# A second, unread result on some VectorE comparisons in an FNet block with a routed feed-forward row

## The chip, the cores and the metric

The kernel runs on one core of one Trainium2 chip. The metric is the device time of one execution in microseconds (us). A change of less than about 2 us (1%) can't be told from none here.

## The reference

```python
h  = x + A(layernorm(x))          # x: [2048, 576] f32
#   A(z) = Re( DFT_seq( DFT_hid(z) ) ), both DFTs given as full cos/sin matrices
h2 = h + B(layernorm(h))
#   B(z): r = z @ w_r; take the one row with the largest r;
#         y = (silu(z_row @ w_gate) * (z_row @ w_up)) @ w_down * sigmoid(r_row)
#         return z, with y added at that row
# seq matrices 2048x2048 (re, im), hid matrices 576x576 (re, im),
# w_gate, w_up 576x4608, w_down 4608x576, all f32
```

## The kernel before, in words

The sequence DFT is done by symmetry: of each 2048-row matrix only some blocks of columns are used in matmuls. A program that relied on the symmetry without looking would be wrong for other inputs, so the kernel also loads the other blocks and compares them with their mirror images: a difference is written as bf16 into a buffer `Q` (two slots), ScalarE squares it and adds it up (`add_square`, L368), and at the end a sum above zero sends the program into a general path that is not run here.

A block `C[j, i, False]` comes straight by a DMA of SP's queue (`load_c`, L357). Its mirror image `C[j, i, True]` has its rows in reverse order, so it comes by an indirect DMA, a gather, whose descriptors GpSimd (POOL) makes (`gather`, L301; 32 such gathers of the sequence matrices, 3 of the hidden matrices, 4 of `x`). Four functions on VectorE (DVE) compare: `off_s` (L375, a block with its mirror), `off_t` (L380, block `NK - j` with block `j` reversed), `off_h` (L387, halves of a block, a subtraction and an addition) and `off_w` (L422 to L427, the hidden matrices). All are `tensor_tensor` with both inputs f32 in SBUF. When a comparison has read its buffer, the buffer goes back to a ring of seven `RAW` and some `D` buffers, and the next load or gather into it can be issued. Between the comparisons DVE also does the steps of the transform: `keep` (L583, one input in PSUM), `residual` (L619) and `dot_h` (L623), the last two with a sum (`accum_out`), which the engine returns by an extra instruction, DVE_READ_ACCUMULATOR.

The order of all this work is written out by a small planner, `Plan`: each step is added with its engine, a duration in us and the steps it depends on; `order()` simulates the engines and returns the steps by start time, and the program is emitted in that order. The dependencies themselves are kept by semaphores. `load` (L705) adds a load on SP or POOL; `c_half`, `c_check` and `w_check` add the comparisons. The feed-forward weights (`load_ffn`, L1200) follow on SP's queue, into buffers as they come free.

Of the kernel before, what the change touches and what calls it, by code (L numbers as in the profile page):

```python
# [7 lines left out]
F32 = mybir.dt.float32  # L8
# [3 lines left out]
OP = mybir.AluOpType  # L12
AX = mybir.AxisListType

P = 128
S = 2048
D = 576
F = 4608
NK = S // P
# [51 lines left out]
class Plan:  # L71
# [3 lines left out]
    def __init__(self):  # L75
        self.ops = []

    def add(self, eng, dur, fn, *deps, tail=0.0, push=0.0):
        flat = []
        for d in deps:  # L80
            flat += d if isinstance(d, list) else [d]
        n = {"eng": eng, "dur": dur, "fn": fn, "deps": [d for d in flat if d], "tail": tail, "push": push}
        n["i"] = len(self.ops)
        self.ops.append(n)
        return n

    def order(self):
        HOP = 0.15
        succ = [[] for _ in self.ops]
        for n in self.ops:  # L90
            for d in n["deps"]:
                succ[d["i"]].append(n)
        for n in reversed(self.ops):
            n["way"] = n["dur"] + n["tail"] + max((m["way"] for m in succ[n["i"]]), default=0.0)
        left = [len(n["deps"]) for n in self.ops]
        open_ = {}
        for n in self.ops:
            n["at"] = 0.0
            if not n["deps"]:
                open_.setdefault(n["eng"], []).append(n)  # L100
        free = {}
        done = []
        while any(open_.values()):
            best = None
            for eng, ns in open_.items():
                if not ns:
                    continue
                t = max(free.get(eng, 0.0), min(n["at"] for n in ns))
                n = min(
                    (n for n in ns if n["at"] <= t + 1e-9),  # L110
                    key=lambda n: (n["at"] if eng == "DMA" else -n["way"] - n["push"], n["i"]),
                )
                if best is None or t < best[0]:
                    best = (t, n)
            t, n = best
            open_[n["eng"]].remove(n)
            n["start"], n["end"] = t, t + n["dur"]
            free[n["eng"]] = n["end"]
            done.append(n)
            for m in succ[n["i"]]:  # L120
                hop = 0.0 if m["eng"] == n["eng"] else HOP
                m["at"] = max(m["at"], n["end"] + n["tail"] + hop)
                left[m["i"]] -= 1
                if not left[m["i"]]:
                    open_.setdefault(m["eng"], []).append(m)
        assert len(done) == len(self.ops)
        return sorted(done, key=lambda n: (n["start"], n["i"]))


class Slots:  # L130
# [12 lines left out]
def kernel(  # L143
# [13 lines left out]
    pe, act, dve, pool, sp = nc.tensor, nc.scalar, nc.vector, nc.gpsimd, nc.sync  # L157
# [23 lines left out]
    mp = main.enter_context(tc.tile_pool(name="main", bufs=1))  # L181
# [4 lines left out]
    eps = consts.tile([P, 1], F32, name="eps")  # L186
# [153 lines left out]
    C, DT = {}, {}  # L340
# [28 lines left out]

    SIGN = (OP.subtract, OP.add)  # L370

    def off_s(j, i, u, n):

        o = Q[:, u % 2, n * 7 * P : (n + 1) * 7 * P].rearrange("p (k m) -> p k m", m=P)
        dve.tensor_tensor(o, C[j, i, True][:, 0:7, :], C[j, i, False][:, 7:0:-1, :], op=SIGN[i])  # L375

    def off_t(j, i, u):

        o = Q[:, u % 2, 14 * P : QW].rearrange("p (k m) -> p k m", m=P)
        dve.tensor_tensor(o, C[NK - j, i, False], C[j, i, False][:, :, ::-1], op=SIGN[i])  # L380

    def off_h(g, c, n, i, u):

        o = Q[:, u % 2, i * 9 * n * HM : (i + 1) * 9 * n * HM].rearrange("p (c k m) -> p c k m", k=9, m=HM)
        t = DT[g, i][:, c : c + n]
        for k, op in enumerate((OP.subtract, OP.add)):
            dve.tensor_tensor(o[:, :, k::2, :], t[:, :, k::2, 0:HM], t[:, :, k::2, HM:P], op=op)  # L387

    def square(u, w, ps=P):
        add_square(Q[0:ps, u % 2, 0:w])  # L390
# [26 lines left out]
    def off_w(n, u):  # L417

        ps = W_ROWS[n]
        t, o = WM["ABC"[n]][0:ps], Q[0:ps, u % 2]  # L420
        re, im = W["ABC"[n]][0:ps, 0, :], W["ABC"[n]][0:ps, 1, :]
        dve.tensor_tensor(o[:, 0:D], t[:, 0:D], re[:, 0:D], op=OP.subtract)  # L422
        dve.tensor_tensor(o[:, D : 2 * D], t[:, D : 2 * D], im[:, 0:D], op=OP.add)
        o = o[:, 2 * D : 3 * D]
        dve.tensor_tensor(o[:, 0:287], re[:, 1:HD], re[:, D - 1 : HD : -1], op=OP.subtract)
        dve.tensor_tensor(o[:, 287:575], im[:, 1 : HD + 1], im[:, D - 1 : HD - 1 : -1], op=OP.add)
        dve.tensor_copy(o[:, 575:576], im[:, 0:1])  # L427
# [264 lines left out]
    plan = Plan()  # L692
    add = plan.add

    def then(f, *args):
        return lambda: f(*args)
# [8 lines left out]
    def load(eng, f, mb, *deps):  # L705

        ns = in_flight[eng]
        n = add(eng, 0.1 if eng == "SP" else 1.3, f, *deps, ns[-8:-7])
        d = add("DMA", mb / 0.405, None, n, moved[-1:])
        moved.append(d)  # L710
        ns.append(add("COME", 0.0, None, d, tail=1.8))
        return n, ns[-1]
# [4 lines left out]
    def in_turn(eng, f, mb, *deps):  # L717
        LAST[eng], d = load(eng, f, mb, LAST[eng], *deps)
        return d
# [6 lines left out]
    for k, n in X_LOADS:  # L726
        d = in_turn("SP" if k < 9 else "POOL", then(load_x, k, n), 0.295 * n)
# [11 lines left out]
    for a, b in X_RUNS:  # L739
        ks = ORDER[a:b]  # L740
        push = 8.0 if a == 14 else 0.0
        e = add("POOL", 0.6, then(ends, a, b), [CAME[k] for k in ks])
        r = [add("DVE", 0.84, then(fold_d, k), CAME[k]) for k in ks]
        m = [add("ACT", 0.95, then(measure, k), f, push=push) for k, f in zip(ks, r)]
        o = add("POOL", 0.3, then(totals, a, b), e, m)
# [3 lines left out]
        o = add("POOL", 2.0, then(biases, a, b), r, o)  # L749
# [23 lines left out]
    for k in FOLDED:  # L773
        dg, use, at = [], [], []
        for sl in slots_of(k):
            n = next(places)
            UF[sl] = LATER[n]
            at.append(PLACE[n])
            if k in PAIRS:
                u, w = dgs.take()  # L780
                dg.append(add("DVE", 0.17, then(diag, sl, u), MEAS[sl], w, IDENT))
                use.append(u)
        if k in PAIRS:
            of = ys if k % 2 else zs
            (y0, w0_), (y1, w1_) = of.take(), of.take()
            f = pe_last = add("PE", 1.95, then(fold, k), dg, w0_, w1_, pe_last)
# [45 lines left out]
    def c_half(g, c, m):  # L832
        u, w = qs.take()
        cus = [[CU[j, i, False] for j in GROUPS[g][c : c + m]] for i in range(2)]
        n = [
            add("DVE", 0.16 + 0.62 * m, then(off_h, g, c, m, i, u), [d for _, d in cus[i]], w)
            for i in range(2)
        ]
        for i in range(2):
            for b, _ in cus[i]:  # L840
                users[b].append(n[i])
        squares(u, 9 * m * P, n)

    def squares(u, w, n, ps=P):
        SQUARES.append(add("ACT", 0.3 + w / 1200, then(square, u, w, ps), n))
        qs.users[u].append(SQUARES[-1])

    def c_check(j, i):

        u, w = qs.take()  # L850
        u0, d0 = CU[j, i, False]
        c_load(j, i, True)
        u1, d1 = CU[j, i, True]
        n = [add("DVE", 1.08, then(off_s, j, i, u, 0), d0, d1, w)]
        users[u0] += n
        users[u1] += n
        free.append(u1)
        if j in PAIRS:
            m = NK - j
            c_load(m, i, False)  # L860
            c_load(m, i, True)
            (u2, d2), (u3, d3) = CU[m, i, False], CU[m, i, True]
            n.append(add("DVE", 1.08, then(off_s, m, i, u, 1), d2, d3, w))
            users[u3].append(n[1])
            n.append(add("DVE", 1.36, then(off_t, j, i, u), d0, d2, w))
            users[u0].append(n[2])
            users[u2] += n[1:]
            free.extend([u3, u2])
        if u0[0] == "D1":
            free.append(u0)  # L870
        squares(u, QW if j in PAIRS else 7 * P, n)

    WS, WL, WRAP = [], [], []
# [8 lines left out]
    def w_check():  # L882
        for n in range(3):
            u, d = ring("POOL", load_w, (0.59, 0.59, 0.16)[n], n + 3)
            q, w = qs.take()
            o = add("DVE", 2.2, then(off_w, n, q), WL[n], d, w)
            users[u].append(o)
            squares(q, 3 * D, o, W_ROWS[n])
            WS.append(o)
            free.append(u)  # L890
# [259 lines left out]
    o = add("DVE", 1.0, check_sum, SCORES, SQUARES, xs_is)  # L1150
    o = add("PE", 0.3, check_all, o)
# [6 lines left out]
    for b in range(NJ // TW):  # L1158
        j = TW * b
# [186 lines left out]
    after, best = {}, None  # L1346
    for _ in range(N_PLAN):
        end, todo, next_ = plan_ffn(after)
        if best is None or end < best[0]:
            best = end, after  # L1350
        after = next_
    for n in plan_ffn(best[1])[1]:
        if n["fn"]:
            n["fn"]()
    main.close()


    with tc.If(T["mv"], preferred_fallthrough_block=False):
        with ExitStack() as gen:
# [33 lines left out]
            with ExitStack() as hs:  # L1393
# [9 lines left out]
                with tc.For_i(0, NK, 1) as k:  # L1403
                    dve.tensor_copy(xr, row_of(GX, k))
                    norm(xn, xr, "x")
                    for a in range(5):
                        w = min(P, D - a * P)
# [4 lines left out]
                    for c in range(4):  # L1412
                        pa = zbank(f"gpa{c}")
                        for a in range(5):
                            w = min(P, D - a * P)
                            pe.matmul(
                                pa[:, :HD], xt[0:w, a, :], GW[0:w, a, c * HD : (c + 1) * HD],
                                start=(a == 0), stop=(a == 4),
# [8 lines left out]
            with tc.For_i(0, NK, 1) as j:  # L1427
                dve.tensor_copy(hn, row_of(GX, j))
                with tc.For_i(0, 2 * NK, NB) as k0:
# [7 lines left out]
                    for k in range(NB):  # L1437
                        for c in range(2):
                            pe.matmul(
                                ps[c][:, :HD], gc[:, k, :], gk[:, k, half(c)],  # L1440
                                start=(k == 0), stop=(k == NB - 1),
# [89 lines left out]
```

## Time and profile before

| | |
|---|---|
| median of 3 runs | 199.22 us (198.27, 199.22, 199.5) |
| the profiled execution | 199.04 us |
| its span, first to last instruction | 197.4 us |
| moved by DMA | 77.81 MB, 394 GB/s over the span |
| busy: DVE, ACT, PE, POOL | 84%, 71%, 66%, 59% |

The span is what the trace shows; 1.64 us of the profiled execution lie around it. Busy shares are means over stages that differ. POOL's busy time includes the time that a gather is held up, since a held gather shows as a long one.

### The profile page before, as it was taken

To read this page: it belongs to the slowest core of one execution; us is meant where nothing else is said; L and a number is where in the kernel's file an instruction comes from. 1 tells how busy PE (TensorE), PEld (TensorE's weight loads), DVE (VectorE), ACT (ScalarE), POOL (GpSimd) and SP (SyncE) were. 2 spreads that over 40 slices of the span, in tenths; PEclk is the share of its full clock that TensorE was granted. 3 is DMA by queue.
4 is the path that set the end of the run, shared out by engine and by line. 5 is a ranking of instruction groups with operands and counts; after the bars stand their busy time and mean duration, and the time that the engine had idled before them with its cause. 6 is when DMAs were issued, how large, how long until landed. Compare 5 with 4: busy or idle time off the path is not lost. (4 is left out here: it accounts for less than half of the span.)

```text
span 197.4 us, 2794 instructions
## 1 busy us (share of the span) xinstructions
PE 129.6 (66%) x758; PEld 89.9 (46%) x758; DVE 166.6 (84%) x419; ACT 140.4 (71%) x259; POOL 117.2 (59%) x139
## 2 busy tenths in 40 slices
PE   0007999999999999799999986900232036263940
PEld 0005667754667788477876764700121013031430
DVE  4399996999899968999799999999947999989720
ACT  3198853684699578799389399889555999877630
POOL 6488888284637876359780000003874999999900
PEclk9999999999999999999999999975555555558797
DMA  5999999999899999999999999999999999999992
GB/s 171 408 418 412 413 409 406 411 381 330 281 405 411 411 363 402 400 410 411 416 405 414 418 424 420 426 422 412 424 431 425 420 428 424 422 431 414 412 427 99
DMA packets 14587, 77.81 MB, mean 394 GB/s; under 512 B 1951, under 2 KB 1955, under 8 KB 11239
## 3 DMA queue, kind: packets, MB, share of 16 engines
q1 hardware_dynamic: 10461, 56.56, 71.5%
q0 software_dynamic: 4096, 21.03, 26.5%
q8 instruction: 7, 0.11, 0.2%
q14 instruction: 13, 0.11, 0.1%
q10 hardware_dynamic: 10, 0.00, 0.0%
HBM read 72.86 MB, written 6.49 MB: 402 GB/s over the span
## 5 line engine op out<-in xcount | busy, mean ns | idle before, releaser
L368 ACT ACTIVATE Q<-Q 128x2944 bf16<-128x2944 bf16 (+5 forms) x26 | 55.4, 2132 | 18.5 <-DVE Q L380 8.9
L610 PE MATMUL py<-W,Z 128*128 128x289 f32 x180 | 45.4, 409 | 3.8 <-DVE X L619 3.8
L565 PE MATMUL ps<-D,XF 128*128 128x320 f32 (+3 forms) x216 | 45.0, 408 | 0.5 <-DVE Z L583 0.5
L301 POOL DMA_INDIRECT R<-in_ct_dram,ic x21 | 32.1, 1528 | 17.7 <-DVE Q L375 13.5
L610 PEld LDWEIGHTS py<-W,Z 128*128 128x128 f32 x180 | 33.6, 189 | 15.2 <-issue 4.5
L565 PEld LDWEIGHTS ps<-D,XF 128*128 128x128 f32 (+1 forms) x216 | 32.0, 172 | 13.0 <-issue 1.5
L1228 POOL TENSOR_TENSOR D<-D,Z 128x1152 f32<-128x1152 f32 x8 | 20.9, 2642 | 0.0
L676 POOL DMA_DIRECT2D out_dram<-X x1 | 0.6, 621 | 32.1 <-ACT X L661 32.1
L301 POOL DMA_INDIRECT D<-in_ct_dram,ic x11 | 13.8, 1250 | 7.6 <-DVE Q L380 4.6
L498 ACT ACTIVATE junk<-X,XT 128x576 bf16<-128x576 f32 x16 | 12.3, 771 | 7.8 <-DMA X<-in_x_dram 3.3
L1233 ACT ACTIVATE junk<-D 128x576 bf16<-128x576 f32 x20 | 13.7, 683 | 3.2 <-POOL D L1228 2.6
L1255 PE MATMUL pd<-XF,H 128*1 128x144 f32 x80 | 5.3, 439 | 14.6 <-DVE H L1247 11.3
L537 PE MATMUL fo<-W,diag 128*128 128x288 f32 (+1 forms) x8 | 4.2, 706 | 16.3 <-DVE diag L528 16.3
L375 DVE TENSOR_TENSOR Q<-R,D 128x896 bf16<-128x896 f32 x11 | 11.9, 1084 | 3.2 <-DMA D<-in_ct_dram 1.8
L387 DVE TENSOR_TENSOR Q<-D 128x640 bf16<-128x640 f32 (+3 forms) x20 | 12.8, 691 | 1.7 <-DMA W<-in_wt_dram 1.7
L380 DVE TENSOR_TENSOR Q<-R,D 128x1152 bf16<-128x1152 f32 x10 | 13.4, 1348 | 0.0
L630 ACT ACTIVATE junk<-X,TD 128x576 bf16<-128x576 f32 x16 | 12.3, 766 | 1.4 <-DVE X L619 1.3
L661 ACT ACTIVATE X<-X,BB,UP 128x576 f32<-128x576 f32 x14 | 10.8, 854 | 3.1 <-DVE BB L642 3.1
L623 DVE SCALAR_TENSOR_TENSOR junk<-X,wr 128x576 bf16<-128x576 f32 x16 | 12.1, 755 | 0.3
L375 DVE TENSOR_TENSOR Q<-D 128x896 bf16<-128x896 f32 x11 | 11.8, 1082 | 0.0
L619 DVE SCALAR_TENSOR_TENSOR X<-py,X 128x576 f32<-128x576 f32 x16 | 11.6, 748 | 0.0
L375 DVE TENSOR_TENSOR Q<-R 128x896 bf16<-128x896 f32 x10 | 10.7, 1082 | 0.1
(205 smaller groups left out, 260.8 us busy)
## 6 DMA issues: line engine op xcount, KB each, us to landing
D<-in_ct_dram SPq DMA_DIRECT2D x22, 576.0 KB
R<-in_ct_dram SPq DMA_DIRECT2D x10, 576.0 KB
D<-in_wu_dram SPq DMA_DIRECT2D x5, 1152.0 KB
D<-in_wd_dram SPq DMA_DIRECT2D x4, 1152.0 KB
R<-in_wg_dram SPq DMA_DIRECT2D x3, 1152.0 KB
D<-in_wg_dram SPq DMA_DIRECT2D x3, 1152.0 KB
out_dram<-X SPq DMA_DIRECT2D x2, 1440.0 KB
X<-in_x_dram SPq DMA_DIRECT2D x4, 576.0 KB
```

Source lines behind the costliest of these rows:

```text
L301: pool.indirect_dma_start(tile, None, view, bass.IndirectOffsetOnAxis(ap=rows, axis=0), element_offset=at)
L368: act.activation(t, t, AF.Square, accum_out=DS[0 : t.shape[0], n : n + 1])
L375: dve.tensor_tensor(o, C[j, i, True][:, 0:7, :], C[j, i, False][:, 7:0:-1, :], op=SIGN[i])
L380: dve.tensor_tensor(o, C[NK - j, i, False], C[j, i, False][:, :, ::-1], op=SIGN[i])
L387: dve.tensor_tensor(o[:, :, k::2, :], t[:, :, k::2, 0:HM], t[:, :, k::2, HM:P], op=op)
L498: act.activation(junk[:, 0:D], X[:, k, 0:D], AF.Square, bias=XT[:, n : n + 1], scale=-float(D), accum_out=VX[:, n : n + 1],)
L565: pe.matmul(cm(ZP[g, n][k % 2][p0 : p0 + m], w), XF[:, q, m0 : m0 + m], DT[g, i][:, :, k, 0:HM], start=k in (0, 1), stop=k in (6, 7),)
L610: pe.matmul(YP[GROUPS[g][c]][:, h, 0:w], Z[:, a, c * P : (c + 1) * P], w_block(a)[:, h * HD : h * HD + w], start=(a == 0), stop=(a == 4),)
L623: dve.scalar_tensor_tensor(junk2, X[:, k, 0:D], 1.0, wr, op0=OP.mult, op1=OP.mult, accum_out=TD[:, n, 0:1])
L630: act.activation(junk[:, 0:D], X[:, k, 0:D], AF.Square, bias=TD[:, n, 1:2], scale=-float(D), accum_out=VAR[:, n : n + 1],)
L1228: pool.tensor_tensor(t, t, xs.unsqueeze(1).to_broadcast([P, JW, D]), op=OP.mult)
L1233: act.activation(junk[:, 0:D], WB[w, j][:, r, :], AF.Copy, accum_out=acc[:, j + r : j + r + 1])
```

## The change

A step can now be marked `holds` (the comparisons of `c_half`, `c_check` and `w_check`) or `moves` (the loads). After the planner has made its order, `apart` goes through the loads on POOL's queue: it looks for the DVE step `a` that is running, by the planner's own times, when the load starts. If `a` holds, the pair of `a` and its successor and the next pair after that are looked at, and the first of a pair is noted if both hold and less than 0.2 us lie between them. The order is made before that and stays as it is; no load, buffer or wait on another engine is changed by the code of the diff.

A noted comparison is emitted as `scalar_tensor_tensor` (multiply by 1.0, then the same subtraction or addition) with `accum_out` into a new two-column tile `spill` that nobody reads. This brings a DVE_READ_ACCUMULATOR behind it. `off_h` keeps its two `tensor_tensor` and gets between them a product of one column, also with a sum. In `off_w` only the first of five operations takes part.

```diff
+    def apart(self, todo):
+        ops = [n for n in todo if n["eng"] == "DVE"]
+        found = set()
+        for n in todo:
+            if n["eng"] != "POOL" or not n["moves"]:
+                continue
+            for k, (a, b) in enumerate(zip(ops, ops[1:])):
+                if a["start"] <= n["start"] + 0.0 < a["end"] and a["holds"]:
+                    for a, b in list(zip(ops, ops[1:]))[k : k + 2]:
+                        if a["holds"] and b["holds"] and b["start"] - a["end"] < 0.2:
+                            found.add(a["i"])
+        return found
...
+    spill = mp.tile([P, 2], F32, name="spill")
+    open_ = [False]
+    def differ(o, a, b, op):
+        if open_[0]:
+            dve.scalar_tensor_tensor(o, a, 1.0, b, op0=OP.mult, op1=op, accum_out=spill[:, 0:1])
+        else:
+            dve.tensor_tensor(o, a, b, op=op)
+    def pause():
+        dve.scalar_tensor_tensor(
+            spill[:, 1:2], eps, 1.0, eps, op0=OP.mult, op1=OP.mult, accum_out=spill[:, 0:1]
+        )
...
-        dve.tensor_tensor(o, C[j, i, True][:, 0:7, :], C[j, i, False][:, 7:0:-1, :], op=SIGN[i])
+        differ(o, C[j, i, True][:, 0:7, :], C[j, i, False][:, 7:0:-1, :], SIGN[i])
...
-        dve.tensor_tensor(o, C[NK - j, i, False], C[j, i, False][:, :, ::-1], op=SIGN[i])
+        differ(o, C[NK - j, i, False], C[j, i, False][:, :, ::-1], SIGN[i])
...
             dve.tensor_tensor(o[:, :, k::2, :], t[:, :, k::2, 0:HM], t[:, :, k::2, HM:P], op=op)
+            if open_[0] and k == 0:
+                pause()
...
-        dve.tensor_tensor(o[:, 0:D], t[:, 0:D], re[:, 0:D], op=OP.subtract)
+        differ(o[:, 0:D], t[:, 0:D], re[:, 0:D], OP.subtract)
...
-    for n in plan_ffn(best[1])[1]:
+    todo = plan_ffn(best[1])[1]
+    apart = plan.apart(todo)
+    for n in todo:
         if n["fn"]:
+            open_[0] = n["i"] in apart
             n["fn"]()
```

## Rows read from the trace of the kernel before

**Rows 1.** The table by stretch: start and end of the stretch and its length in us, busy time of each engine (and its instructions), the granted TensorE clock, the mean busy share of the 16 DMA engines, and what they moved. A share may read slightly above 1.

```profile
44.00:48.00 4.00, 4.00 (x31) 1.99 (x29) 3.48 (x5) 2.00 (x5) 0.94 (x1) 1.00 1.04 288
...
50.50:54.00 3.50, 3.50 (x15) 2.47 (x14) 2.55 (x5) 2.91 (x3) 2.26 (x2) 1.00 0.81 237
54.00:72.00 18.00, 18.00 (x74) 13.41 (x73) 16.09 (x19) 15.13 (x18) 11.92 (x9) 1.00 1.02 410
...
76.00:104.00 28.00, 26.47 (x126) 20.68 (x126) 26.23 (x42) 21.45 (x27) 18.21 (x14) 1.00 1.02 409
104.00:172.00 68.00, 32.36 (x204) 21.27 (x198) 62.79 (x172) 55.20 (x113) 30.99 (x29) 0.69 1.01 422
172.00:192.00 20.00, 11.88 (x196) 6.33 (x196) 14.35 (x47) 12.78 (x38) 15.40 (x6) 0.76 1.02 422
```

**Rows 2.** The timeline of SP's queue, from three windows: start and length in us, line, operation, target and source; the last row is the last load of feed-forward weights.

```profile
41.72 0.33 SPq L357 DMA_DIRECT2D R<-in_ct_dram  x1
51.02 0.33 SPq L357 DMA_DIRECT2D R<-in_ct_dram  x1
171.09 0.33 SPq L1202 DMA_DIRECT2D W<-in_wd_dram  x1
```

**Rows 3.** Who waited for whom, SP's queue, 44 to 52 us: total, times, longest.

```profile
SPq L357 <- DVE Q L380: 8.9, 1, 8.9
```

**Rows 4.** POOL's timeline, gathers only: start, length; in brackets the idle time before it and what ended that.

```profile
39.69 4.30 POOL L301 DMA_INDIRECT R<-in_ct_dram,ic  x1 [3.49 <-DVE Q L375]
44.29 0.94 POOL L301 DMA_INDIRECT R<-in_ct_dram,ic  x1 [0.30 <-DVE bt L737]
48.20 1.55 POOL L301 DMA_INDIRECT R<-in_ct_dram,ic  x1 [2.96 <-DVE Q L375]
50.06 1.76 POOL L301 DMA_INDIRECT R<-in_ct_dram,ic  x1 [0.31 <-DVE Z L583]
52.12 0.95 POOL L301 DMA_INDIRECT R<-in_ct_dram,ic  x1 [0.30 <-issue]
55.23 1.55 POOL L301 DMA_INDIRECT R<-in_ct_dram,ic  x1 [2.16 <-DVE Q L375]
...
88.20 4.33 POOL L301 DMA_INDIRECT R<-in_ct_dram,ic  x1 [0.30 <-issue]
...
95.75 1.29 POOL L301 DMA_INDIRECT R<-in_ct_dram,ic  x1 [0.30 <-issue]
```

**Rows 5.** DVE's timeline beside the first of these gathers and up to the fifth, in the same columns. Lengths of neighbours overlap by 0.08 us; the time that an operation takes is from its start to the next start.

```profile
39.34 1.08 DVE L375 TENSOR_TENSOR Q<-R 128x896 bf16<-128x896 f32 x1
40.34 1.35 DVE L380 TENSOR_TENSOR Q<-R,D 128x1152 bf16<-128x1152 f32 x1
41.61 1.55 DVE L387 TENSOR_TENSOR Q<-D 128x320 bf16<-128x320 f32 x4
43.09 0.88 DVE L583 SCALAR_TENSOR_TENSOR Z<-ps,os 128x320 f32<-128x320 f32 x2
...
44.57 1.09 DVE L375 TENSOR_TENSOR Q<-R,D 128x896 bf16<-128x896 f32 x1 [0.52 <-ACT Q L368]
...
49.65 1.34 DVE L380 TENSOR_TENSOR Q<-R,D 128x1152 bf16<-128x1152 f32 x1
50.91 1.08 DVE L375 TENSOR_TENSOR Q<-D 128x896 bf16<-128x896 f32 x1
...
53.87 1.09 DVE L375 TENSOR_TENSOR Q<-R,D 128x896 bf16<-128x896 f32 x1 [0.95 <-ACT Q L368]
54.88 1.08 DVE L375 TENSOR_TENSOR Q<-D 128x896 bf16<-128x896 f32 x1
55.88 1.35 DVE L380 TENSOR_TENSOR Q<-D 128x1152 bf16<-128x1152 f32 x1
```

**Rows 6.** DVE's timeline beside the gather at 88.20.

```profile
87.67 0.75 DVE L619 SCALAR_TENSOR_TENSOR X<-py,X 128x576 f32<-128x576 f32 x1
88.35 0.08 DVE L619 DVE_READ_ACCUMULATOR X<-py,X 128x1 f32 x1
88.35 1.08 DVE L375 TENSOR_TENSOR Q<-D 128x896 bf16<-128x896 f32 x1
89.36 1.34 DVE L380 TENSOR_TENSOR Q<-R,D 128x1152 bf16<-128x1152 f32 x1
90.62 1.08 DVE L375 TENSOR_TENSOR Q<-R 128x896 bf16<-128x896 f32 x1
91.63 0.74 DVE L583 SCALAR_TENSOR_TENSOR Z<-ps,os 128x256 f32<-128x256 f32 x2
```

**Rows 7.** Groups of instructions by line and shape: busy us, mean ns of one.

```profile
L623 DVE SCALAR_TENSOR_TENSOR junk<-X,wr 128x576 bf16<-128x576 f32 x16 | 12.1, 755 | 0.3
...
L423 DVE TENSOR_TENSOR Q<-R,W 128x576 bf16<-128x576 f32 x1 | 0.8, 754 | 0.0
```

**Rows 8.** DVE's timeline where a small operation and sums with their readings follow one another.

```profile
131.58 0.15 DVE L642 SCALAR_TENSOR_TENSOR BB<-TD,RS 128x6 f32<-128x6 f32 x1
131.66 0.75 DVE L623 SCALAR_TENSOR_TENSOR junk<-X,wr 128x576 bf16<-128x576 f32 x1
132.33 0.08 DVE L623 DVE_READ_ACCUMULATOR junk<-X,wr 128x1 f32 x1
132.44 0.76 DVE L623 SCALAR_TENSOR_TENSOR junk<-X,wr 128x576 bf16<-128x576 f32 x1
```

More of the change, by code (lines that the diff above doesn't have):

```diff
@@ L76, in __init__, with add @@
         self.ops = []
-    def add(self, eng, dur, fn, *deps, tail=0.0, push=0.0):
+    def add(self, eng, dur, fn, *deps, tail=0.0, push=0.0, holds=False, moves=False):
         flat = []
@@ L82, in add @@
         n = {"eng": eng, "dur": dur, "fn": fn, "deps": [d for d in flat if d], "tail": tail, "push": push}
+        n["holds"], n["moves"] = holds, moves
         n["i"] = len(self.ops)
@@ L707, in load @@
         ns = in_flight[eng]
-        n = add(eng, 0.1 if eng == "SP" else 1.3, f, *deps, ns[-8:-7])
+        n = add(eng, 0.1 if eng == "SP" else 1.3, f, *deps, ns[-8:-7], moves=True)
         d = add("DMA", mb / 0.405, None, n, moved[-1:])
@@ L835, in c_half @@
         n = [
-            add("DVE", 0.16 + 0.62 * m, then(off_h, g, c, m, i, u), [d for _, d in cus[i]], w)
+            add("DVE", 0.16 + 0.62 * m, then(off_h, g, c, m, i, u), [d for _, d in cus[i]], w, holds=True)
             for i in range(2)
@@ L853, in c_check @@
         u1, d1 = CU[j, i, True]
-        n = [add("DVE", 1.08, then(off_s, j, i, u, 0), d0, d1, w)]
+        n = [add("DVE", 1.08, then(off_s, j, i, u, 0), d0, d1, w, holds=True)]
         users[u0] += n
@@ L862, in c_check @@
             (u2, d2), (u3, d3) = CU[m, i, False], CU[m, i, True]
-            n.append(add("DVE", 1.08, then(off_s, m, i, u, 1), d2, d3, w))
+            n.append(add("DVE", 1.08, then(off_s, m, i, u, 1), d2, d3, w, holds=True))
             users[u3].append(n[1])
-            n.append(add("DVE", 1.36, then(off_t, j, i, u), d0, d2, w))
+            n.append(add("DVE", 1.36, then(off_t, j, i, u), d0, d2, w, holds=True))
             users[u0].append(n[2])
@@ L885, in w_check @@
             q, w = qs.take()
-            o = add("DVE", 2.2, then(off_w, n, q), WL[n], d, w)
+            o = add("DVE", 2.2, then(off_w, n, q), WL[n], d, w, holds=True)
             users[u].append(o)
```

## The prediction

> **What bounds the kernel now.** I read the table by stretch first, because one number in it is the same nearly everywhere: the DMA engines are busy all the time and move 410 GB/s or so [rows 1]. From 54 us to 192 us they hardly pause: 410, 409, 422 and 422 GB/s in the stretches shown. The bytes are fixed, so the end can only move if the engines get more done before 54 us, or if they run dry later. For the second, look at SP's queue: its last load of weights is issued at 171.09 [rows 2], and the engines are busy with such loads until 192 [rows 1], so there are some 20 us of issued work in hand at the end. Nothing that DVE or POOL does a few us sooner or later in the last third is seen in the time.
>
> What remains are two holes. From 44 to 48 us the engines are busy (1.04) but move only 288 GB/s: their packets are slow, not missing. From 50.5 to 54 they are really short of work: a share of 0.81 and 237 GB/s [rows 1]. Against 410 GB/s the holes are worth (410 - 288) x 4 / 410 = 1.2 us and (410 - 237) x 3.5 / 410 = 1.5 us, together 2.7 us. This is all that better feeding could give in the stretch where the first long gather lies.
>
> Who feeds the second hole? SP issues a load at 41.72 and the next at 51.02 [rows 2]; it waits 8.9 us for DVE's comparison L380 [rows 3], the one that starts at 49.65 and is over at 50.91 [rows 5]. So the hole ends when DVE has worked its way to that comparison.
>
> **What holds the gathers.** An undisturbed gather takes 0.95 us (the one at 52.12) [rows 4]. The one at 39.69 takes 4.30: it ends at 43.99, which is 0.90 after 43.09, where DVE goes over from comparisons with two SBUF inputs to L583, which has one in PSUM [rows 4, 5]. The one at 88.20 ends at 92.53, again 0.90 after such a step (91.63) [rows 4, 6]. So a gather waits for DVE, and needs some 0.9 us from its release. Others are held too, but only to the next seam: the one at 55.23 lies in L375, whose successor L380 also has two SBUF inputs, and ends at 56.78, 0.90 after the seam at 55.88 [rows 4, 5]. No reading stood in that seam. The one at 95.75 is also held for a little only (1.29 us). Two gathers, then, missed seams of a kind that lets others through, and the rows don't show why.
>
> **What the change does, part by part.**
>
> *Which comparisons are noted.* The planner's own times decide, but the trace has the same order, so I put the gathers' starts among DVE's rows. The gather at 39.69 starts in L375 at 39.34; its successors L380 and L387 also hold; so L375 and L380 are noted. The gather at 55.23 notes L375 and L380 likewise. The gather at 48.20 starts in an L375 in front of L583 and notes nothing. The gather at 88.20 starts in L619 (87.67 to 88.35), which is not of the marked kind, so nothing is noted there, though this is the second of the long ones [rows 4 to 6]. If the planner puts it 0.15 us later, it is noted. Over all gathers of the page I count some 14 noted comparisons that way; I take 14, with 5 and 30 as ends, as the planner's times are not the chip's.
>
> *What is gained on POOL.* If the reading works as a seam, the gather at 39.69 is let go at 40.34 and ends at 40.34 + 0.90 = 41.24, so 2.75 us sooner, and the one at 44.29 follows it (0.30 us behind) at about 41.5. The third, at 48.20, waits for DVE [rows 4] and stays. At 88.20 the gain would be 91.63 - 89.36 = 2.27 us if noted. All other gathers are already let go at the first seam, and a reading there gives nothing. So POOL gains 2.75 us, at most 5.
>
> *Who gains from that.* Two gathers' data come up to 2.75 us sooner, about 44 to 48 us. No row shows DVE waiting for them: its two idle times up to 54 us are for ACT's squares (0.52 and 0.95) [rows 5]. SP's load at 51.02 waits for DVE, not for POOL. So the same work is served sooner, in the stretch where the packets are slow, and the hole that follows is no shorter: what is moved forward is missing later, until SP's load of 51.02 sets in. I cost the gain at zero. It is covered by the wait for L380; if that cover were gone, up to the 2.7 us of both holes could come back.
>
> After 76 us the engines are full whatever the order of their work, so an earlier gather at 88.20 only goes ahead of a load of SP.
>
> *What is paid on DVE.* A comparison turned into `scalar_tensor_tensor` with a sum: the nearest row is L623, f32 inputs in SBUF, bf16 output, a sum; 755 ns against 754 ns for a `tensor_tensor` of the same shape [rows 7]. So the rate is the same. Its reading costs nearly nothing: behind L619 the next operation starts in the same moment as the reading (88.35) [rows 6], at most 0.01 us. But where the next operation writes the same tile as the one before, it starts 0.11 us after the reading (132.33 to 132.44: L623 writes `junk2` each time) [rows 8]. Two noted comparisons in a row both write `spill`, so I charge 0.11 us to the second. A `pause` in `off_h` is one small operation, 0.08 us from start to start (131.58 to 131.66) [rows 8], and 0.11 us if `spill` was just written: 0.19.
>
> *The sum.* What counts is what lies on DVE's way to 50.91, where SP's load is let go. Noted there: L375 at 39.34, L380 at 40.34 and, for the gather that starts in it at 50.06 [rows 4], L380 at 49.65 [rows 5]. That is 3 x 0.01 + 1 x 0.11 = 0.14 us. DVE's wait for ACT at 44.57 [rows 5] may absorb some of it; I don't count on that. If the planner also notes four of the `off_h` in front of 43.09, 4 x 0.19 = 0.76 comes on top: 0.9 us as the upper end. The lower end is the gain of 2.7 us. I take 0.14, as three comparisons are what the rows show. The noted comparisons after 54 us (some 11, about 11 x 0.01 + 5 x 0.11 = 0.7 us of DVE) lie beside a DMA that has work in hand and cost nothing.
>
> The profiled execution took 199.04 us (197.4 of span, 1.64 around), 0.18 below the median of 199.22. 199.04 + 0.14 = 199.18, or 199.36 against the median. I say 199.3.
>
> **The rivals.**
>
> *Faster: the holes are filled.* For it: a gather's packets mixed with the slow ones from 44 to 48 us may raise the rate there, and data that come sooner may let something start that the rows put down to another cause, since a wait for several semaphores is put down to the last. Against it: the hole at 50.5 us ends by a wait for DVE [rows 3]. It gives up to 2.7 us: 199.3 - 2.7 = 196.6. It is over 1% from three quarters of that on.
>
> *The change doesn't do what it says.* The reading at 88.35 stands right in front of L375, with the gather already started at 88.20, and it was not let through there [rows 4, 6]. If a reading is no seam, the gather at 39.69 still ends near 44 and only the cost remains: 199.3. In time this can't be told from the forecast; in the trace it can.
>
> *Slower: the comparison with a sum runs at half the rate.* The place is L375 and L380 at 39.34 and 40.34 and L380 at 49.65, before SP's load is let go. At double time the first two cost 40.34 - 39.34 + 41.61 - 40.34 = 2.27 us, and the third 1.26 (49.65 to 50.91) [rows 5], together 3.5 us, all of it on the way to 51.02: the hole grows by it. Since the hole costs time one for one, the end comes at 199.3 + 2.27 = 201.6 if two of them are noted and at 202.8 with three. It decides from about 1.9 us extra on the way to 50.91 on. Against it stands the row of L623: 755 ns, no more than a plain operation [rows 7]; for it, that no row has these shapes, reversed in one input, with a sum.
>
> [...]
>
> **How the numbers follow.** The forecast, with the rival that the change does nothing (the same time), 0.68. Faster by over 1% (2 us, about what a measurement of this kernel can tell from no change) 0.18: the mechanism is possible, its ceiling is only 2.7 us, and the row of SP's wait speaks against it. Slower by over 1% 0.14: a doubled duration is unlikely by the row of L623, but more marks than counted or another lengthening on DVE's way to 50.91 end at the same place. The range goes from the filled holes, 196.6, to two doubled comparisons, 201.6, and leaves out little more than what neither bound covers.
>
> **What would show it.** Right: the gather near 39.7 ends near 41.3 instead of 43.99, the next one near 42.5; SP's load that was at 51.02 comes at 51.0 to 51.3; the stretch from 50.5 to 54 still shows a share near 0.8; from 54 on the rates are those of before. The noted comparisons last 1.08 and 1.35 us with a reading of 0.08 behind them. Wrong: SP's load before 50 us, or a rate well above 288 GB/s from 44 to 48 with no deeper hole behind it (the faster rival); comparisons of 2 us and more (the slower one); a gather near 39.7 that still lasts over 4 us (no seam). What would also make it wrong is a planner that notes other comparisons than the trace suggests, above all many `off_h` before 43 us.

## The result, and the profile after

The changed kernel takes 200.03 us (median of 9 runs, 199.64 to 201.1) against 198.56 (197.86 to 199.5) of the kernel before beside it: a ratio of 1.0074, interval 1.0046 to 1.0102. That is within 1%, but not nothing: about 1.5 us slower, and the interval doesn't contain 1.0: nine executions each can tell apart less than the 2 us named at the start. Medians and ranges here and below are of all executions; the ratios leave out those more than 1.5% above the fastest of their kernel. The profiled execution took 200.32 us with a span of 198.5, 1.1 more than before.

In the trace of the kernel after the comparisons of `off_s` and `off_t` and the first of `off_w` stand at two lines: L394 with a sum (noted) and L396 without. L399 is a `pause`, L418 `off_h`. L317 is a gather, L373 `load_c`, L616 `keep`, L652 `residual`, L1233 `load_ffn`; in the runs with fills on POOL these lines are three higher. Seventeen comparisons and three `pause`s are noted; with their readings DVE has 23 instructions more. First the head of the page, with busy time by engine:

```profile
span 198.5 us, 2817 instructions
PE 129.9 (65%) x758; PEld 89.6 (45%) x758; DVE 167.7 (85%) x442; ACT 140.6 (71%) x259; POOL 109.6 (55%) x139
```

POOL is busy 55% instead of 59%: the 32 gathers that start between 30 and 104 us take 37.9 us together instead of 45.7. The first place, POOL's gathers and DVE's rows near 39 us:

```profile
38.48 1.55 POOL L317 DMA_INDIRECT R<-in_ct_dram,ic  x1 [2.47 <-DVE Q L396]
40.33 1.10 POOL L317 DMA_INDIRECT R<-in_ct_dram,ic  x1 [0.30 <-issue]
...
38.13 1.08 DVE L394 SCALAR_TENSOR_TENSOR Q<-R 128x896 bf16<-128x896 f32 x1
39.14 0.07 DVE L394 DVE_READ_ACCUMULATOR Q<-R 128x1 f32 x1
39.25 1.36 DVE L394 SCALAR_TENSOR_TENSOR Q<-R,D 128x1152 bf16<-128x1152 f32 x1
```

The gather that lasted 4.30 us [rows 4] now ends at 40.03, which is 0.89 after the reading at 39.14. (A second trace of the kernel before, below, has 1.56 us at this place without any reading.) The second place, near 88 us:

```profile
87.22 0.94 POOL L317 DMA_INDIRECT R<-in_ct_dram,ic  x1 [0.30 <-issue]
88.46 0.95 POOL L317 DMA_INDIRECT D<-in_ct_dram,ic  x1 [0.30 <-issue]
89.72 0.96 POOL L317 DMA_INDIRECT D<-in_ct_dram,ic  x1 [0.30 <-issue]
91.14 0.95 POOL L317 DMA_INDIRECT R<-in_ct_dram,ic  x1 [0.46 <-DVE Q L396]
...
87.37 0.08 DVE L652 DVE_READ_ACCUMULATOR X<-py,X 128x1 f32 x1
87.37 1.08 DVE L394 SCALAR_TENSOR_TENSOR Q<-D 128x896 bf16<-128x896 f32 x1
88.38 0.08 DVE L394 DVE_READ_ACCUMULATOR Q<-D 128x1 f32 x1
...
96.53 1.09 DVE L394 SCALAR_TENSOR_TENSOR Q<-R,D 128x896 bf16<-128x896 f32 x1 [3.98 <-DMA D<-in_ct_dram]
```

Here too the long gather of before (4.33 us at 88.20 [rows 4]) is gone, and three more gathers follow it before 92 us. The last row is the new thing: DVE stands still for 3.98 us until a load of SP has landed. The row of before at this place:

```profile
95.14 1.09 DVE L375 TENSOR_TENSOR Q<-R,D 128x896 bf16<-128x896 f32 x1 [1.77 <-DMA D<-in_ct_dram]
```

So DVE goes on at 96.53 instead of 95.14. Who had the DMA engines in the meantime? From the answer on DMA queues for 88 to 96 us (packets, MB, the time of their packets as a share of 16 engines), first before:

```profile
q1 hardware_dynamic: 596, 2.45, 76.4%
q0 software_dynamic: 152, 0.85, 26.1%
```

then after:

```profile
q1 hardware_dynamic: 446, 1.82, 57.2%
q0 software_dynamic: 259, 1.46, 44.8%
```

q1 carries SP's loads, q0 the gathers: from 115 to 134 us of the kernel before, where no gather runs, q1 has 101.1% and q0 isn't listed. The gathers have 44.8% of the engines instead of 26.1%, SP's loads 57.2% instead of 76.4%, and the sum stays full (102.0 and 102.5%).

The rest of the way is in SP's timeline: the load of weights that waits until the row's products have freed a buffer. Before, then after:

```profile
155.06 0.35 SPq L1200 DMA_DIRECT2D R<-in_wu_dram  x1
```
```profile
156.71 0.35 SPq L1233 DMA_DIRECT2D R<-in_wu_dram  x1
```

What SP waited for there, in the kernel before (total, times, longest): first DVE's products of the row, then those of ScalarE.

```profile
SPq L1200 <- DVE junk L1217: 5.9, 2, 5.8
SPq L1200 <- ACT junk L1233: 3.7, 5, 1.1
```

And in the table by stretch, in the columns of [rows 1], again before and then after:

```profile
156.00:172.00 16.00, 6.30 (x96) 2.98 (x96) 15.54 (x38) 14.94 (x42) 16.00 (x8) 0.50 1.01 424
```
```profile
54.00:72.00 18.00, 18.00 (x74) 13.55 (x73) 16.24 (x28) 14.06 (x18) 12.23 (x11) 1.00 1.02 400
...
76.00:104.00 28.00, 24.85 (x111) 18.94 (x111) 23.95 (x42) 19.75 (x25) 13.99 (x13) 1.00 1.02 408
104.00:172.00 68.00, 33.76 (x214) 22.07 (x210) 62.61 (x172) 55.35 (x109) 29.34 (x28) 0.71 1.00 412
...
156.00:172.00 16.00, 6.29 (x96) 2.94 (x96) 15.51 (x41) 15.22 (x42) 16.00 (x7) 0.50 0.99 388
```

From 156 to 172 us it moves 388 GB/s instead of 424: (424 - 388) x 16 / 424 = 1.4 us of DMA time, more than the 1.1 us of span. Narrower, 154 to 170 us in 40 slices of 0.4 us, it is a notch; the kernel after:

```profile
DMA  9998999869699999998999999998999999999999
GB/s 438 426 438 357 472 415 433 369 265 357 207 300 311 392 392 392 415 415 277 415 392 438 392 392 369 369 300 323 392 392 461 438 392 438 415 392 484 438 392 415
```

Between 157 and 159 us the rate falls to as little as 207 GB/s, and the share to 0.6 in two of the slices. The kernel before has no slice below 369 there.

### The profile page after: what moved, and what is told of

It reads as the page before. It is cut to its first block, busy times and chain, and to the rows that moved or that the text cites. A ratio compares the mean times of both kernels' runs of the same rounds, so it can differ in the third digit from the quotient of the medians.

```text
span 198.5 us, 2817 instructions
## 1 busy us (share of the span) xinstructions
PE 129.9 (65%) x758; PEld 89.6 (45%) x758; DVE 167.7 (85%) x442; ACT 140.6 (71%) x259; POOL 109.6 (55%) x139
## 4 chain that ended last, share of the span: by engine, by line
DVE 31%; issue 18%; DMA 17%; PE 15%; POOL 15%; ACT 0%; SPq 0%; POOLq 0%; DVEq 0%
DVE Q L396 8%; DMA D<-in_ct_dram 7%; DMA D<-in_wt_dram,iw 6%; POOL D L1261 6%; DVE junk L656 6%; PE ps L598 5%; PE fo L570 4%; DMA X<-in_x_dram,ix 4%; DVE X L652 4%; POOL R L317 3%; DVE Q L418 3%; PE pd L1288 2%; DVE Z L616 2%; PE fe L570 2%; PE spin L1298 2%
## 5 line engine op out<-in xcount | busy, mean ns | idle before, releaser
L317 POOL DMA_INDIRECT R<-in_ct_dram,ic x21 | 26.5, 1264 | 25.6 <-DVE Q L396 13.7
L709 POOL DMA_DIRECT2D out_dram<-X x1 | 0.6, 621 | 33.5 <-ACT X L694 33.5
L317 POOL DMA_INDIRECT D<-in_ct_dram,ic x11 | 11.7, 1061 | 7.6 <-DVE Q L396 4.6
L396 DVE TENSOR_TENSOR Q<-R,D 128x896 bf16<-128x896 f32 (+1 forms) x12 | 14.3, 1197 | 1.4 <-ACT Q L384 1.4
L394 DVE SCALAR_TENSOR_TENSOR Q<-R,D 128x1152 bf16<-128x1152 f32 (+1 forms) x9 | 11.1, 1236 | 4.2 <-DMA D<-in_ct_dram 4.0
L1288 PE MATMUL pd<-XF,H 128*1 128x144 f32 x80 | 4.8, 398 | 14.4 <-DVE H L1280 11.3
L396 DVE TENSOR_TENSOR Q<-D 128x896 bf16<-128x896 f32 (+1 forms) x12 | 13.6, 1151 | 0.0
L418 DVE TENSOR_TENSOR Q<-D 128x640 bf16<-128x640 f32 (+3 forms) x20 | 13.1, 695 | 0.4 <-DMA D<-in_ct_dram 0.4
L652 DVE SCALAR_TENSOR_TENSOR X<-py,X 128x576 f32<-128x576 f32 x16 | 11.6, 752 | 0.0
L271 PE MATMUL pmt<-ident,gt 128*128 128x128 f32 x4 | 1.2, 454 | 13.8 <-DVE gt L276 13.8
```

What stands on the lines that cost most here:

```text
L317: pool.indirect_dma_start(tile, None, view, bass.IndirectOffsetOnAxis(ap=rows, axis=0), element_offset=at)
L396: dve.tensor_tensor(o, a, b, op=op)
L652: dve.scalar_tensor_tensor(t, y, 1.0, t, op0=OP.mult, op1=OP.add, accum_out=TD[:, n, 1:2])
```

## The experiments

Three theories stood. **A**: near 88 us the gathers come sooner, their data take the engines from a load that DVE needs near 95 us; DVE is late from there on, the row's products too, the reloads at 155 us come late, and the DMA engines have a hole. **B**: the twenty sums and readings themselves make DVE late. **C**: the new tile `spill` shifts other tiles, and that costs. The steps 350 and 358 named below are the two noted comparisons near 88 us (87.37 and 88.50).

**Only the two near 88 us.**

```diff
     apart = plan.apart(todo)
+    apart &= {350, 358}
```

> Of the twenty noted comparisons only two stay noted, the L394 pair that runs from 87 to 90 us, beside the gather that was long in the kernel before (4.33 us). Theory A (the gather let go there puts gathers' data ahead of a load of SP that VectorE needs; VectorE waits 4.0 instead of 1.8 us for it; everything behind comes later, and the loads that follow the chosen row come too late for the DMA engines near 157 us): the gather lasts 0.95 to 1.4 us, VectorE's wait near 93 us is 3 to 4 us, and the ratio to the kernel before is 1.004 to 1.010, as for the whole change. Theory B (the twenty sums and readings themselves slow VectorE): 1.000 to 1.002.

Measured: 198.99 us (198.39 to 199.88), ratio 1.0047 (1.0022 to 1.0072). The gather at 85.48 takes 2.05 us. DVE's timeline:

```profile
86.64 0.08 DVE L394 DVE_READ_ACCUMULATOR Q<-D 128x1 f32 x1
...
95.79 1.09 DVE L396 TENSOR_TENSOR Q<-R,D 128x896 bf16<-128x896 f32 x1 [5.00 <-DMA D<-in_ct_dram]
```

The gather ends at 87.53, 0.89 after the reading at 86.64; so the reading lets it go. A had expected 0.95 to 1.4 us for this gather and a wait of 3 to 4 us on DVE; they are 2.05 and 5.00. The gathers have 55.1% of the engines from 88 to 96 us, the reload comes at 155.65, and 156 to 172 us moves 393 GB/s. Two sums bring 0.47% where twenty bring 0.74% (the intervals overlap), and B allowed 0.2% at most: A.

**All but these two.**

```diff
+    apart -= {350, 358}
```

> The other eighteen stay noted, those two are plain again. Theory A: a gather near 87 us lasts over 4 us as before, VectorE's wait near 93 us is back under 2.5 us, and the ratio is 0.995 to 1.002. Theory B: 1.005 to 1.008, nearly as for the whole change.

Measured: 199.69 us (198.51 to 201.41), ratio 1.0069 (1.0031 to 1.0107). By the edit alone this speaks for B. The trace says why A's number was missed: the gather wasn't held although the comparisons around it are plain. POOL, then DVE:

```profile
86.62 0.94 POOL L317 DMA_INDIRECT R<-in_ct_dram,ic  x1 [0.31 <-issue]
...
86.77 0.08 DVE L652 DVE_READ_ACCUMULATOR X<-py,X 128x1 f32 x1
86.77 1.08 DVE L396 TENSOR_TENSOR Q<-D 128x896 bf16<-128x896 f32 x1
...
96.17 1.09 DVE L394 SCALAR_TENSOR_TENSOR Q<-R,D 128x896 bf16<-128x896 f32 x1 [4.37 <-DMA D<-in_ct_dram]
```

It took 0.94 us, like one that isn't held, though it started 0.15 us ahead of that comparison, just as the held one of before did (88.20 and 88.35 [rows 4, 6]). The rest is A's chain again: gathers 56.4% of the engines, reload at 156.05, 404 GB/s. The run doesn't part A from B.

**The same form without sum and reading.**

```diff
-            dve.scalar_tensor_tensor(o, a, 1.0, b, op0=OP.mult, op1=op, accum_out=spill[:, 0:1])
+            dve.scalar_tensor_tensor(o, a, 1.0, b, op0=OP.mult, op1=op)
```

(and likewise in `pause`)

> All twenty are still scalar_tensor_tensor, but without the sum, so no reading stands behind them. If the reading is what lets a gather through (theory A needs that): two gathers last over 4 us again, near 39 and near 87 us, and the ratio is 0.997 to 1.002. If the other form of instruction alone does it: no gather over 2 us, and the ratio is 1.004 to 1.010. Theory B: between 1.000 and 1.004, as only the readings and their waits are gone.

Measured: 199.53 us (197.84 to 203.22), ratio 1.0048 (1.0012 to 1.0084). Its profiled execution was the longest of its runs (203.22), so I read only the seams from it. POOL, then DVE:

```profile
90.38 4.32 POOL L317 DMA_INDIRECT R<-in_ct_dram,ic  x1 [0.30 <-issue]
...
91.53 1.34 DVE L394 SCALAR_TENSOR_TENSOR Q<-R,D 128x1152 bf16<-128x1152 f32 x1
92.80 1.07 DVE L396 TENSOR_TENSOR Q<-R 128x896 bf16<-128x896 f32 x1
93.80 0.74 DVE L616 SCALAR_TENSOR_TENSOR Z<-ps,os 128x256 f32<-128x256 f32 x2
```

The gather misses the seams at 91.53 and 92.80 and ends at 94.70, 0.90 after 93.80. Near 39 us a gather is held as well; near 55 us one gets through a seam of this form (at 55.82, by its end at 56.72):

```profile
39.63 3.23 POOL L317 DMA_INDIRECT R<-in_ct_dram,ic  x1 [3.63 <-DVE Q L396]
55.17 1.55 POOL L317 DMA_INDIRECT R<-in_ct_dram,ic  x1 [2.16 <-DVE Q L396]
```

One trace is thin here, so I counted in all twelve, for gathers of 1.1 us or more that start between 30 and 110 us, which seam lies 0.89 us ahead of the gather's end. A reading behind a comparison let the gather go 20 times out of 20. The new form without a sum did so at 1 seam of 11 (this run), and all seams between two comparisons without a reading together, these included, at 57 of 106. So it is the reading that ends the hold each time, not the other instruction. The ratio missed what A expected (0.997 to 1.002), and this trace doesn't explain it.

**Only the early ones** (before 42 us).

```diff
+    apart &= {165, 166, 171, 184, 185}
```

> Only the five noted steps before 42 us stay noted (three halves with a small product between, and the pair beside the first long gather). Theory A: that gather is let go (1.0 to 1.6 us), the one near 88 us is long again, VectorE's wait near 93 us is under 2.5 us, and the ratio is 0.993 to 1.001, below 1 if the earlier data in the holes from 44 to 54 us is worth something. Theory B: 1.001 to 1.003, a quarter of the whole.

Measured: 199.86 us (198.0 to 201.88), ratio 1.0067 (1.003 to 1.0105). A had expected 1.001 at most. In its trace, which is of the shortest execution (198.0), the gather near 88 us is held (4.32 us), DVE waits 0.73 us and goes on at 93.74, the reload comes at 153.94, and 156 to 172 us moves 425 GB/s with a span of 196.3: nothing of the loss is to be seen there. The gather may have been let go in others, but that isn't shown. This time stays open.

**The tile alone.**

```diff
-    apart = plan.apart(todo)
+    apart = set()
```

> The changed kernel with none noted: the tile spill is there, no comparison is different from the kernel before. All four parts of the change tried so far cost 0.5 to 0.7%, which a common cause would explain. Theory C (the new tile moves others in memory, or the code of it, and that costs): 1.004 to 1.008. Theory A (a gather let go near 87 us goes ahead of a load that VectorE needs; without readings it is let go in some executions and held in others): 0.998 to 1.002, as the kernel before.

Measured: 198.61 us, ratio 0.9995 (0.9961 to 1.0028); gather 4.33 us, 34.6% of the engines for gathers, reload 153.93, 425 GB/s. C falls.

**The kernel before once more**, for a second trace of it.

> The kernel before once more, for a second trace and for the spread. 0.998 to 1.002. Theory A: the lengths of the gathers near 39 and 88 us need not be those of the first trace; if the one near 88 us is under 2 us here, VectorE's wait near 93 us is 3 us or more and the rate from 156 to 172 us is under 410 GB/s, and if it is over 3 us, the wait is under 2.5 us and the rate over 415.

Measured: 198.9 us, ratio 1.0014 (0.9977 to 1.0051). Gather 4.33 us, 33.5%, reload 153.90. But the hole from 50.5 to 54 us isn't there:

```profile
50.50:54.00 3.50, 3.50 (x14) 2.47 (x13) 2.54 (x4) 3.50 (x3) 1.33 (x2) 1.00 1.01 397
```

and the gather near 39 us takes 1.56 us without any sum. The 4.30 us and the 237 GB/s [rows 1, 4] belonged to that execution, not to the kernel.

**All sums, and the gather made late** by six fills of `junk2` on POOL, 3.78 us, ahead of it.

```diff
+        if mirror and (j, i) == (0, 0):
+            for _ in range(6):
+                pool.memset(junk2, 0.0)
```

> The whole change, with six fills of an unused scratch tile on GpSimd (some 3 us) ahead of the gather near 87 us, so that this gather and those behind it come as late as where the gather was held. Theory A: VectorE's wait near 93 us is under 2.5 us, the rate from 156 to 172 us is over 415 GB/s, and the ratio is 0.993 to 1.002, at or under the kernel before although all sums are still paid. Theories B and C: 1.005 to 1.010, as for the change alone.

Measured: 198.37 us (198.05 to 200.39), ratio 0.9995 (0.9959 to 1.003). DVE's and SP's timeline:

```profile
94.81 1.09 DVE L397 SCALAR_TENSOR_TENSOR Q<-R,D 128x896 bf16<-128x896 f32 x1 [3.65 <-DMA D<-in_ct_dram]
...
154.69 0.35 SPq L1236 DMA_DIRECT2D R<-in_wu_dram  x1
```

All twenty sums are there, and their cost is gone: B falls. The gather starts at 89.48, gathers have 36.4% of the engines, 156 to 172 us moves 425 GB/s. The wait of 3.65 us missed what I expected (under 2.5): DVE was 1.4 us ahead of the kernel after already at the seam of `residual` (85.98 against 87.37) and waited for what it had won. Counted from that seam, DVE goes on after 8.83 us here, 9.16 in the kernel after and 6.79 in the kernel before: most of the early 94.81 is this head start. So the run speaks against B, but shows little of A's first step; the one with three fills does that.

**The kernel before, with DVE late behind all this**: seven fills, 2.85 us, ahead of the row search.

```diff
+    def late_start():
+        for _ in range(7):
+            dve.memset(junk2.bitcast(F32), 0.0)
+        T["steps"][0]()
-    step = add("DVE", 0.25, T["steps"][0], SCORES)
+    step = add("DVE", 0.25, late_start, SCORES)
```

> The kernel before, with seven fills of a scratch tile on VectorE (some 1.8 us) ahead of the first step of the search for the row, near 141 us; nothing ahead of it is different. It measures what a late VectorE costs there. Theory A: loads that wait for the row's products (155.06 us before) come 1.8 us later, the rate from 156 to 172 us falls under 412 GB/s, and the ratio is 1.003 to 1.010. If there is work in hand for the DMA engines, as the prediction took it: 0.999 to 1.002.

Measured: 201.11 us (200.35 to 202.38), ratio 1.0141 (1.0097 to 1.0185). The timelines of DVE and SP, and the table by stretch:

```profile
141.62 2.85 DVE L1116 MEMSET junk<- 128x288 f32 x7
...
157.56 0.35 SPq L1205 DMA_DIRECT2D R<-in_wu_dram  x1
```

```profile
156.00:172.00 16.00, 6.29 (x96) 2.96 (x96) 15.48 (x41) 15.27 (x43) 16.00 (x8) 0.50 0.98 381
```

The gather near 88 us is as before (4.33 us). The ratio lies above what A expected (1.003 to 1.010), since the fills took 2.85 us and not 1.8. 1.41% is 2.8 us (1.9 to 3.7 by the interval) for 2.85 us of fills: a late DVE at the row search is paid about one for one, with no gather in it. This is the second half of A by itself.

**All sums, half the delay**: three fills, 1.86 us.

```diff
+            for _ in range(3):
```

> As the run with six fills on GpSimd ahead of the gather near 87 us, with three (half the delay). If that delay is what pays the loss back (theory A), the effect goes with its size: VectorE resumes after its wait for the load between 94.8 (six fills) and 96.5 us (none), the loads behind the row's products begin between 154.7 and 156.7 us, and the ratio to the kernel before lies between 1.000 and 1.006. If the fills do something else (a chance of order): a ratio over 1.006 or under 0.998.

Measured: 198.92 us, ratio 1.0012 (0.9983 to 1.0041). DVE's timeline:

```profile
88.64 0.08 DVE L655 DVE_READ_ACCUMULATOR X<-py,X 128x1 f32 x1
...
95.04 1.09 DVE L397 SCALAR_TENSOR_TENSOR Q<-R,D 128x896 bf16<-128x896 f32 x1 [1.23 <-DMA D<-in_ct_dram]
```

This run has no head start: DVE passes the seam of `residual` at 88.64, 1.3 us later than in the kernel after, and still goes on at 95.04, 1.5 us sooner and only 6.40 us after that seam. Reload at 154.90, 425 GB/s.

**The kernel after once more.**

> The changed kernel once more, for a second trace and for the spread beside the same runs of the kernel before. Theory A: ratio 1.004 to 1.010; the gather near 87 us is let go again (under 2.1 us), VectorE resumes near 96 us or later, and the loads behind the row's products begin at 156 us or later, at a rate under 412 GB/s from 156 to 172 us.

Measured: 200.71 us (199.12 to 201.12), ratio 1.0087 (1.0051 to 1.0123); gather 0.95 us at 88.11, gathers 52.3% of the engines, DVE waits 4.27 us and goes on at 97.70, reload at 157.57, 404 GB/s. The same chain in a second trace. The run with three fills was measured beside this one: the same twenty sums, intervals that don't overlap, and only the gather near 88 us and those behind it made later.

Set side by side (e3 left out):

| | gather near 88: us | gathers' share 88 to 96 | DVE goes on | reload | GB/s 156 to 172 | ratio |
|---|---|---|---|---|---|---|
| before | 4.33 | 26% | 95.14 | 155.06 | 424 | 1 |
| tile only | 4.33 | 35% | 94.08 | 153.93 | 425 | 0.9995 |
| before again | 4.33 | 34% | 94.04 | 153.90 | 425 | 1.0014 |
| six fills | 0.95, at 89.48 | 36% | 94.81 | 154.69 | 425 | 0.9995 |
| three fills | 1.73, at 90.23 | 36% | 95.04 | 154.90 | 425 | 1.0012 |
| early only | 4.32 | 31% | 93.74 | 153.94 | 425 | 1.0067 |
| two late | 2.05 | 55% | 95.79 | 155.65 | 393 | 1.0047 |
| all but two | 0.94 | 56% | 96.17 | 156.05 | 404 | 1.0069 |
| after | 0.94 | 45% | 96.53 | 156.71 | 388 | 1.0074 |
| after again | 0.95 | 52% | 97.70 | 157.57 | 404 | 1.0087 |
| DVE late at the row | 4.33 | 34% | 94.29 | 157.56 | 381 | 1.0141 |

Reloads up to 155.06 leave the rate at 424 or 425; from 155.65 on it is 381 to 404. In ten of the eleven rows this parts the times as well; the row of the early ones is the exception. One distance hardly changes: the reload comes 59.85 to 60.20 us after DVE goes on, in the ten rows without fills on DVE, and 63.27 with the 2.85 us of fills. And the span ends 41.5 to 43.0 us after the reload in all eleven. So what DVE loses near 95 us arrives whole at the reload and nearly whole at the end.

## Why the prediction was right or wrong

The time came inside the range and the direction was right: no change beyond 1%. I gave +0.14 us; it is +1.1 in the profile and +1.5 in the medians. That 199.3 lies only 0.7 us from 200.03 is in part luck: the median of before that it starts from, 199.22, is 0.66 above that of the nine executions. Point by point:

- *The seams*: right where a gather was held. It ends 0.89 us after the reading (39.14 to 40.03), where I had said 0.90, and so do all twenty counted above (0.89 to 0.90). But the 2.75 us that I gave to POOL were not the reading's: the second trace of before has a short gather there too. The rival that a reading is no seam falls for readings behind a comparison; those behind `residual` let go none of the eight held gathers that met one.
- *The comparisons' price*: right. The groups by shape in the kernel after:

```profile
L394 DVE SCALAR_TENSOR_TENSOR Q<-R,D 128x1152 bf16<-128x1152 f32 x5 | 6.8, 1357 | 0.2
...
L396 DVE TENSOR_TENSOR Q<-R,D 128x1152 bf16<-128x1152 f32 x5 | 6.7, 1353 | 0.0
```

  1357 ns with the sum, 1353 without. No run shows the half rate that the slower rival reckons with, so that rival falls. The 0.11 us between two noted ones is there as well (88.38 to 88.50, 0.12). The runs with six and three fills (ratios 0.9995 and 1.0012) show that all of it together isn't seen in the time.
- *SP's load behind L380*: the wait was right, 8.9 us for the comparison, as in [rows 3]. But it comes at 49.95, and "before 50 us" was my sign for the faster rival. The other sign for it, more than 288 GB/s from 44 to 48 us with no deeper hole behind, is there as well:

```profile
44.00:48.00 4.00, 4.00 (x31) 2.00 (x28) 4.00 (x5) 0.95 (x4) 0.87 (x1) 1.00 1.03 332
50.50:54.00 3.50, 3.50 (x14) 2.47 (x13) 2.54 (x5) 3.50 (x3) 1.18 (x2) 1.00 1.01 353
```

  These signs were bad ones, as the kernel isn't faster: the second trace of before has that load at 49.41, and 322 and 397 GB/s in these stretches. The sign for being right, "from 54 on the rates are those of before", did fail: 412 instead of 422 GB/s from 104 to 172 us.
- *The two holes*: the hole at 50.5 us, which my upper bound for a gain came from, isn't a property of the kernel (397 GB/s in its second trace). It took nothing from the forecast, but the faster rival was worth less than I gave it.
- *Which are noted*: 20 instead of 14. Ahead of SP's load it is five, three of them `pause`s, and not L380 at 49.65; by my own prices 3 x 0.19 + 2 x 0.01 + 0.11 = 0.7 us instead of 0.14, within the upper end that I gave. Noted is also the pair near 88 us, as I had said it would be if the planner put that gather 0.15 us later. In the kernel after, though, the gather didn't need it: it wasn't held (0.94 us) and ended at 88.16, before that pair's first reading at 88.38. With only that pair noted, the reading was what let it go.
- *The step that failed*: "After 76 us the engines are full whatever the order of their work, so an earlier gather at 88.20 only goes ahead of a load of SP." It does go ahead of such a load, and that was costed at nothing. But the load was one that DVE waits for, 1.77 us already in the trace of before; I didn't ask whose it was. Behind it stands the wider sentence, "Nothing that DVE or POOL does a few us sooner or later in the last third is seen in the time". I took the 20 us between the last load at 171.09 and the end [rows 1, 2] for a cushion all along the last third. At 155 us there is almost none: the reload waits for the row's products, comes some 60 us after DVE goes on in every trace without fills there, and the run with DVE late there pays 2.8 us for 2.85.
- So the gathers' new order near 88 us, which has no term in the sum, is what was mis-sized: 0 forecast, 1.4 us of DMA time measured from 156 to 172 us.

What stays open: why a gather gets through some seams between such operations and not others (near 88 us, started 0.15 us ahead of the comparison each time, it wasn't held in the three traces whose comparisons between 50 and 86 us carry sums, two of the kernel after and the one with all but two, and was held in the seven without them), and the times of the runs with the early ones alone and without sums. Both of these were slower than before by 0.5 to 0.7%, and neither trace shows the chain. No kernel of these was faster than before; with six or three fills the change is level with it.

## What to carry to other kernels

When gathers are let go sooner while the DMA engines are full (here 102% of 16 engines from 88 to 96 us), ask whose transfer is pushed back: read the next wait for a DMA on every engine (here DVE's, 3.98 us instead of 1.77), not the mean rate. A cushion read from the last issued load, here at 171.09 us, didn't hold at 155 us: 2.85 us of delay on DVE ahead of it cost 2.8. Look for each load that waits for a computation, and whether other loads are still in hand at that moment. And a hole or a long instruction seen in one trace should be looked for in a second one before a bound is built on it (here 237 and 397 GB/s, 4.30 and 1.56 us).

## What the runs showed of the hardware

A gather's instruction on POOL can last until DVE has come to the end of a comparison with two f32 inputs in SBUF, or of several of them in a row: near 88 us one lasts up to 4.33 us, where an undisturbed one takes 0.95 [rows 4], and in four of the runs' traces (the kernel before again among them) another near 62 us lasts 5.6 to 6.6 us:

```profile
61.26 6.58 POOL L301 DMA_INDIRECT D<-in_wt_dram,iw  x1 [0.30 <-issue]
```

A reading of an accumulator behind a comparison ended the hold 20 times out of 20, and the gather ended 0.89 to 0.90 us after it; the same instruction without a sum did so at 1 seam of 11. Where DVE went over from a comparison to `keep` or `residual`, with an input in PSUM, the gather was let go 66 times out of 67. That a gather held up for 4.33 us can be worth more to this kernel than one let go at once (0.94 us) was what I had not expected: it keeps 1.46 - 0.85 = 0.6 MB of the gathers' data out of the way of SP's load from 88 to 96 us.
